# Retention attention and top-1 MoE on one core: score products on array quarters without the masked quarter, value halves swapped by ScalarE, head weights loaded two chunks later

## The chip, the cores and the metric

One Trainium2 chip, of which the kernel uses 1 core. The metric is device microseconds of one execution, as the median of the runs shown; a profile is one profiled execution with its own time. The engines are named as in the profile: PE is TensorE's matrix product and PEld its load of weights, ACT is ScalarE, DVE is VectorE, POOL is GpSimd, and SP (SyncE) issues most transfers. A line Lnnn is a line of the kernel.

## The reference

Four batches of eight heads, 768 positions, head size 64: a decaying linear attention with a causal recurrence. Its output, 3072 rows of 512, goes into a mixture of eight experts, of which each row uses the one with the largest logit.

```python
gamma = 1.0 - 2.0 ** (-5.0 - np.arange(H))            # one decay per head
for t in range(S):
    state = gamma[None, :, None, None] * state + np.einsum('bhd,bhe->bhde', k[:, :, t], v[:, :, t])
    y[:, :, t] = np.einsum('bhd,bhde->bhe', q[:, :, t], state) / np.sqrt(D)

x = y.transpose(0, 2, 1, 3).reshape(B * S, H * D)     # 3072 x 512
logits = x @ w_gate;  e_idx = argmax(logits)          # 8 experts
gate_w = softmax(logits)[e_idx];  eom = sigmoid(x @ w_output_gate)
out[row] = gate_w * eom[e_idx] * (relu(x @ w1[e_idx]) @ w2[e_idx])   # 512 -> 1024 -> 512
```

## The kernel before

The attention is done in chunks of 128 positions. There are 24 of them: chunk i is batch i // 6, position c = i % 6 in it. Queries are laid out for blocks of 256 positions, n = i // 2, so that an even chunk is the first and an odd one the second of its block. Within a chunk the recurrence is written as products: scores of each key with each query, a mask that keeps the keys which are not behind the query, scores times values, and, for c > 0, the query times the state that the chunk before left. The decay is put into the values and into a scale of the result (`gv`, `gq`).

`attend(i, between, before_state)` is one chunk. On TensorE it does, in this order:

- the scores `s` (L331): for each of four head pairs g and each half hh, keys (64 features by 128 keys) with 128 queries, in fp32, which takes two passes. Two such products stand beside each other in the array, each on a half of its rows (64*128 in the profile). VectorE multiplies the result with the mask into `am` (L335), 128x512 for each half hh;
- the carry-in (L348): the state `sd` with the queries, on array quarters (64*64), into `py`. It is left out where c = 0;
- what `between` holds: for even chunks the routing logits of the block before (`logits`, L379, whose result ScalarE copies as `lt`, L382), the transposes of the next chunk's keys (`kt_block`, L286, copied by ScalarE in L288) and of queries (`qt_block`, L304 and L305), then, for even chunks, transposes of the logits (L404) with the routing on VectorE (`route1`, L406 to L421) and an exponential on ScalarE (L425), for odd ones the counting products (L460, L461); and `tokens(i - 3)` (L453), the transposes `px` of finished rows;
- scores times values, onto `py` (L353), and the new state `st` (L361), both on column halves (128*64). The state isn't needed for c = 5.

Then `before_state` puts work of other blocks on the engines: gates of the block before (odd chunks), `build_row(i - 3)`, of which ScalarE writes the row (L506), and `qr_block(i + 3)`, by which ScalarE rearranges queries (L295). Behind it ScalarE copies the state as `sd` (L365) for the next chunk's carry-in, and VectorE multiplies `py` with `gq` into `yt` (L369). There is one buffer for `py`, so the next carry-in waits for `yt`. GpSimd makes the decayed values `vs` (`prep_v(i + 2)`, L281), parts of the rows, and scatters finished rows to memory, sorted by expert (L513).

From chunk 12 on, halves of the first expert's weights are loaded (`load_weights`, at the chunks in the table `w_at`) and, two and three chunks later, split into a high and a low part (`split_weights`: two casts on ScalarE, L176 and L177, two subtractions on GpSimd, L180 and L181). Behind the chunks the first 256 rows of the most frequent expert are computed on TensorE between the last pieces of routing (the head: `head_load`, L577, and `run_head`, L609 and L627), and then come the eight experts (L877, L895).

The order of instructions on PE, ACT, DVE and POOL is the order in which the code is written (`manual_schedule`). Each engine takes its own instructions strictly in that order; only the order of SP's transfers is set by a scheduler.

Of the kernel before, what the change touches and what calls it, by code (L numbers as in the profile page):

```python
# [32 lines left out]
def retention_moe_kernel(  # L33
# [40 lines left out]
    mask = cpool.tile([P, P], F32, name="mask")  # L74
    nc.gpsimd.memset(mask, 1.0)
    nc.gpsimd.affine_select(out=mask.rearrange("p (r m) -> p r m", r=2), in_=mask.rearrange("p (r m) -> p r m", r=2),
                            pattern=[[1, 2], [2, P // 2]], compare_op=ALU.is_ge,
                            fill=0.0, base=0, channel_multiplier=-1)
# [42 lines left out]
    wgs = cpool.tile([2 * NG, P * E], F32, name="wgs")  # L121
# [71 lines left out]
    with ExitStack() as actx:  # L193
# [88 lines left out]

        def kt_block(i):
# [30 lines left out]
        def attend(i, between, before_state):  # L314
# [10 lines left out]
            pss = []  # L325
            for hh in range(2):
                pss.append(ps_s.tile([P, NG, P], F32, name=f"s{hh}", tag="s"))
            for g in range(NG):
                for hh in range(2):
                    r = slice(hh * 64, hh * 64 + 64)  # L330
                    nc.tensor.matmul(rm(pss[hh][:, g]), kt[i][r, g], qc(r, g), start=True, stop=True)  # L331
            am = []
            for hh in range(2):
                a = ap.tile([P, NG, P], F32, name=f"am{hh}", tag=f"am{hh}", bufs=1)
                nc.vector.tensor_tensor(out=a, in0=pss[hh], in1=mask.unsqueeze(1).broadcast_to([P, NG, P]), op=ALU.mult)  # L335
                am.append(a)
# [14 lines left out]
            for g in range(NG):  # L351
                for hh in range(2):
                    nc.tensor.matmul(yo(g, hh), vs[i][:, 2 * g + hh], am[hh][:, g],  # L353
                                     start=(c == 0 and g % 2 == 0), stop=True, skip_group_check=True)
# [8 lines left out]
            before_state()  # L363
            if c < NC - 1:
                nc.scalar.copy(sd[(i + 1) % 2], st)  # L365
            kn.pop(i), vs.pop(i), kt.pop(i)
# [198 lines left out]
        w_at = {12: 0, 14: 2, 16: 4, 18: 6}  # L565
# [8 lines left out]
        def head_load():  # L574
            t = hpool.tile([P, HEAD // 32, SEG], F32, name="xl0")
# [78 lines left out]
        kt_block(0)  # L654
        qr_block(0)
# [10 lines left out]
        for i in range(NCH):  # L666
# [24 lines left out]
            def between():  # L691
# [35 lines left out]
            def before_state():  # L727
                if i == 0:
                    qr_block(2)
# [4 lines left out]
                if i >= 3:  # L734
                    build_row(i - 3)
                if i + 3 < NCH:
# [42 lines left out]
        flush(len(backlog))  # L779

# [326 lines left out]
```

## Time and profile before

| | |
|---|---|
| runs | 444.99, 446.6, 446.89 us |
| median | 446.6 us |
| the profiled execution: its time | 447.45 us |
| the profiled execution: its span | 445.7 us |
| chunks 0 to 2 | 0 to 31.4 us |
| chunks 3 to 23 | 31.4 to 138.0 us |
| the head | 138.0 to 168.6 us |
| the experts | 168.6 to 445.7 us |
| VectorE's mask product (L335) | 48 of 686 ns |
| the copy of the state (L365) | 20 of 375 ns |
| GpSimd's product `vs` (L281) | 24 of 1049 ns |
| casts of weights (L176, whole kernel) | 64 of 621 ns |

A row of the timeline gives the start of a group of like instructions, its busy time, engine, line, operation, output and inputs, the tile of the array (PE), the shapes, the number of instructions, and in brackets how long the engine stood idle before and what ended that. A group of several starts with its first and is busy until its last ends, so that the next may start before it is over: how far two starts lie apart says how long a group keeps its engine. A row of the waits gives the waiting engine and line, what it waited for, the total in us, the number of waits and the longest.

### The profile page before, as it was taken

To read this page: it belongs to the slowest core of one execution; us is meant where nothing else is said; L and a number is where in the kernel's file an instruction comes from. 1 tells how busy PE (TensorE), PEld (TensorE's weight loads), DVE (VectorE), ACT (ScalarE), POOL (GpSimd) and SP (SyncE) were. 2 spreads that over 40 slices of the span, in tenths; PEclk is the share of its full clock that TensorE was granted. 3 is DMA by queue.
4 is the path that set the end of the run, shared out by engine and by line. 5 is a ranking of instruction groups with operands and counts; after the bars stand their busy time and mean duration, and the time that the engine had idled before them with its cause. 6 is when DMAs were issued, how large, how long until landed. Compare 5 with 4: busy or idle time off the path is not lost.

```text
span 445.7 us, 9948 instructions
## 1 busy us (share of the span) xinstructions
PE 429.4 (96%) x3586; PEld 394.8 (89%) x3586; DVE 252.9 (57%) x675; ACT 191.3 (43%) x392; POOL 187.5 (42%) x242
## 2 busy tenths in 40 slices
PE   8999999999999998999999999999999999999993
PEld 4888778777877898999999999999999999999882
DVE  1357766766777538564745475476476476476111
ACT  3235555567764223543533453353343453454111
POOL 4433166458988305106005702711730740720722
PEclk9979999999999999899999999999999999999999
DMA  8949999999951277358444834943953863870102
GB/s 199 231 110 259 240 265 300 273 272 245 266 136 73 82 152 212 128 173 212 128 131 136 223 103 136 252 138 103 247 174 95 219 208 96 224 197 4 54 13 71
DMA packets 110068, 75.52 MB, mean 169 GB/s; under 512 B 55459, under 2 KB 97447, under 8 KB 110008
## 3 DMA queue, kind: packets, MB, share of 16 engines
q1 hardware_dynamic: 104720, 62.03, 54.6%
q0 software_dynamic: 5120, 12.69, 8.7%
q8 instruction: 30, 0.49, 0.5%
q14 instruction: 30, 0.25, 0.2%
q10 hardware_dynamic: 168, 0.06, 0.1%
HBM read 59.41 MB, written 15.83 MB: 169 GB/s over the span
## 4 chain that ended last, share of the span: by engine, by line
issue 44%; POOL 14%; PE 3%; DMA 2%; DVE 0%; POOLq 0%
POOL out_dram L185 14%; PE a L627 2%; PE h L609 1%; DMA out_dram<-ot,idi 1%; DMA out_dram<-ot,idx 1%; DVE ot L639 0%; POOLq L185 0%; DVE a L829 0%; DVE tj L802 0%; DVE no L803 0%; POOLq L979 0%
## 5 line engine op out<-in xcount | busy, mean ns | idle before, releaser
L185 POOL DMA_INDIRECT out_dram<-ot,idi x84 | 88.6, 1055 | 157.1 <-DVE ot L901 133.7
L877 PE MATMUL h<-xh,whi 128*128 128x224 f32 (+7 forms) x256 | 86.3, 337 | 0.0
L877 PE MATMUL h<-xw,whi 128*128 128x224 f32 (+7 forms) x256 | 86.2, 337 | 0.0
L877 PE MATMUL h<-xh,wlo 128*128 128x224 f32 (+7 forms) x256 | 86.2, 337 | 0.0
L895 PE MATMUL a<-hh,whi 128*128 128x224 f32 (+6 forms) x224 | 75.5, 337 | 1.1 <-ACT hh L881 1.1
L895 PE MATMUL a<-hl,whi 128*128 128x224 f32 (+6 forms) x224 | 75.7, 338 | 0.3 <-DVE hl L882 0.3
L895 PE MATMUL a<-hh,wlo 128*128 128x224 f32 (+6 forms) x224 | 75.5, 337 | 0.0
L180 DVE TENSOR_TENSOR wlo<-raw,whi 128x512 fp32r<-128x512 f32 x56 | 38.3, 684 | 58.8 <-ACT whi L176 55.8
L176 ACT CAST whi<-raw 128x512 fp32r<-128x512 f32 x64 | 39.8, 621 | 70.7 <-PE a L895 69.0
L882 DVE SCALAR_TENSOR_TENSOR hl<-h,hh 128x224 fp32r<-128x224 f32 (+7 forms) x64 | 34.9, 546 | 55.7 <-ACT hh L881 55.7
L881 ACT ACTIVATE hh<-h 128x224 fp32r<-128x224 f32 (+7 forms) x64 | 30.9, 485 | 79.2 <-PE h L877 79.1
L877 PEld LDWEIGHTS h<-xh,whi 128*128 128x128 f32 x256 | 48.6, 190 | 0.8
L877 PEld LDWEIGHTS h<-xw,whi 128*128 128x128 f32 x256 | 48.5, 190 | 0.7
L877 PEld LDWEIGHTS h<-xh,wlo 128*128 128x128 f32 x256 | 48.5, 189 | 0.5
L895 PEld LDWEIGHTS a<-hh,whi 128*128 128x128 f32 x224 | 42.6, 190 | 1.7 <-ACT hh L881 1.2
L895 PEld LDWEIGHTS a<-hl,whi 128*128 128x128 f32 x224 | 42.6, 190 | 1.0 <-DVE hl L882 0.5
L895 PEld LDWEIGHTS a<-hh,wlo 128*128 128x128 f32 x224 | 42.6, 190 | 0.4
L177 ACT CAST whi<-raw 128x512 fp32r<-128x512 f32 x64 | 39.5, 618 | 0.0
L513 POOL DMA_INDIRECT srt<-row,posi x24 | 24.5, 1019 | 33.4 <-ACT sd L365 11.1
L281 POOL TENSOR_TENSOR vs<-vn,gv 128x512 f32<-128x512 f32 x24 | 25.2, 1049 | 31.4 <-DMA vn<-in_v_dram 16.3
L181 DVE TENSOR_TENSOR wlo<-raw,whi 128x512 fp32r<-128x512 f32 x56 | 38.3, 684 | 0.0
L335 DVE TENSOR_TENSOR am<-s,mask 128x512 f32<-128x512 f32 x48 | 30.9, 686 | 9.8 <-PE s L331 9.8
(168 smaller groups left out, 667.4 us busy)
## 6 DMA issues: line engine op xcount, KB each, us to landing
raw<-in_moe_w_dram SPq DMA_DIRECT2D x32, 512.0 KB
raw<-in_moe_w_dram SPq DMA_DIRECT2D x32, 256.0 KB
raw<-in_moe_w_dram SPq DMA_DIRECT2D x64, 128.0 KB
kn<-in_k_dram SPq DMA_DIRECT2D x24, 256.0 KB
qn<-in_q_dram SPq DMA_DIRECT2D x12, 512.0 KB
vn<-in_v_dram SPq DMA_DIRECT2D x24, 256.0 KB
srt<-zrow SPq DMA_DIRECT2D x8, 325.0 KB
xl<-srt SPq DMA_DIRECT2D x12, 211.2 KB
```

What stands on the lines that cost most here:

```text
L176: nc.scalar.copy(cols(hi), r1)
L177: nc.scalar.copy(perm(hi), r2)
L180: eng.tensor_sub(cols(lo), r1, cols(hi).bitcast(F32))
L181: eng.tensor_sub(perm(lo), r2, perm(hi).bitcast(F32))
L185: st = nc.gpsimd.indirect_dma_start(out=dst, out_offset=bass.IndirectOffsetOnAxis(ap=idx, axis=0), in_=src, in_offset=None, bounds_check=n ...
L281: nc.gpsimd.tensor_mul(vs[i], vn.pop(i), gv[:, c, :].unsqueeze(2).broadcast_to([P, H, D]))
L335: nc.vector.tensor_tensor(out=a, in0=pss[hh], in1=mask.unsqueeze(1).broadcast_to([P, NG, P]), op=ALU.mult)
L513: st = nc.gpsimd.indirect_dma_start(out=srt, out_offset=bass.IndirectOffsetOnAxis(ap=posi, axis=0), in_=row, in_offset=None, bounds_check= ...
L877: nc.tensor.matmul(ps[:, 0:C], l[:, 0, w], r[:, dc, 0:C], start=(n == 0), stop=(n == 3 * NDC - 1))
L881: nc.scalar.activation(hh, ps[:, 0:C], AF.Relu)
L882: nc.vector.scalar_tensor_tensor(out=hl, in0=ps[:, 0:C], scalar=0.0, in1=hh.bitcast(F32), op0=ALU.max, op1=ALU.subtract)
L895: nc.tensor.matmul(accs[d][:, 0:C], l[:, 1, w], r, start=(f == 0 and n == 0), stop=(f == NF - 1 and n == 2))
```

## The change

**Scores.** The 128 keys and 128 queries of a chunk are cut into halves of 64. Early queries with late keys are masked altogether, and that quarter isn't computed any more. Early keys (z = 0) are multiplied with all 128 queries, late keys (z = 1) with the late 64 only, all on array quarters (64*64), 16 products in place of 8. For the head pairs 2 and 3 the two key halves land on swapped partitions (`half`). The result takes six blocks of 64 columns, the mask three, and VectorE's product is 128x384 in place of 128x512.

**Values.** The late queries take all 128 keys on column halves (64 columns each). The early queries take the early 64 keys only, on quarters, and come behind the state. Since half of the heads have their keys on swapped partitions, they need their values swapped in the same way: `swap_v` makes `vw`, two copies of 64x256 on ScalarE for each chunk. `before_state` moves behind the early queries' products (but for the last chunk, where it stays and a product of 8 columns, `pd`, is added).

**Order.** `swap_v(i + 1)` stands between `row` and `qr`, so ahead of `sd`, in ScalarE's order; that for chunk 0 stands ahead of the first `qr` and `qt` copies. Chunks 1 and 2 get a product of 8 columns each (`pd`). The table `w_at` moves by two chunks, and the last half's split goes behind the last scatters. The staging tile of the gate weights shares its buffer with the head's first tokens.

```diff
-    mask = cpool.tile([P, P], F32, name="mask")
+    mask = cpool.tile([P, 3, 64], F32, name="mask")
     nc.gpsimd.memset(mask, 1.0)
-    nc.gpsimd.affine_select(out=mask.rearrange("p (r m) -> p r m", r=2), ...
+    for half, x, n in ((0, 0, 1), (0, 2, 1), (1, 0, 2)):
+        m = mask[half * 64:half * 64 + 64, x:x + n].rearrange("p b (r m) -> p b r m", r=2)
+        nc.gpsimd.affine_select(out=m, in_=m, pattern=[[0, n], [1, 2], [2, 32]], compare_op=ALU.is_ge,
+                                fill=0.0, base=0, channel_multiplier=-1)
...
+        def swap_v(i):
+            vw[i] = ap.tile([P, H // 2, D], F32, name="vw", tag="vw", bufs=2)
+            for hf in range(2):
+                nc.scalar.copy(vw[i][64 * hf:64 * hf + 64], vs[i][64 - 64 * hf:P - 64 * hf, H // 2:])
+        def value(i, h):
+            return vs[i][:, h] if h < H // 2 else vw[i][:, h - H // 2]
...
-            for g in range(NG):
-                for hh in range(2):
-                    r = slice(hh * 64, hh * 64 + 64)
-                    nc.tensor.matmul(rm(pss[hh][:, g]), kt[i][r, g], qc(r, g), start=True, stop=True)
+            for g in range(2):
+                for z in range(2):
+                    for gg in (g, g + 2):
+                        for hh in range(2):
+                            r = slice(hh * 64, hh * 64 + 64)
+                            p = half(gg, z)
+                            if z == 0:
+                                out_ = pss[hh][p, g:gg + 3:gg + 2 - g].rearrange("p h (r m) -> p h r m", r=2)
+                                nc.tensor.matmul(out_, kt[i][r, gg, z * 64:z * 64 + 64], halves(qc(r, gg)), ...)
+                            else:
+                                nc.tensor.matmul(rm(pss[hh][p, gg + 2]), kt[i][r, gg, z * 64:z * 64 + 64], halves(qc(r, gg))[:, 1], ...)
...
             between()
-                    nc.tensor.matmul(yo(g, hh), vs[i][:, 2 * g + hh], am[hh][:, g],
-                                     start=(c == 0 and g % 2 == 0), stop=True, skip_group_check=True)
+                    nc.tensor.matmul(halves(rm(yo(g, hh)))[:, 1], value(i, 2 * g + hh), rm(am[hh][:, 2 + g]),
+                                     start=(c == 0 and g % 2 == 0), stop=False, skip_group_check=True)
...
-            before_state()
+            if i == NCH - 1:
+                before_state()
+                nc.tensor.matmul(ps_t.tile([P, NG, P], F32, name="pd", tag="t")[:, 0, 0:E], ident, ident[:, 0:E], start=True, stop=True)
+            for g in range(2):
+                for gg in (g, g + 2):
+                    for hh in range(2):
+                        p = half(gg, 0)
+                        nc.tensor.matmul(halves(rm(yo(gg, hh)))[:, 0], value(i, 2 * gg + hh)[p], rm(am[hh][p, g]),
+                                         start=False, stop=True, skip_group_check=True)
+            if i < NCH - 1:
+                before_state()
             if c < NC - 1:
                 nc.scalar.copy(sd[(i + 1) % 2], st)
...
-        w_at = {12: 0, 14: 2, 16: 4, 18: 6}
+        w_at = {14: 0, 16: 2, 18: 4, 20: 6}
...
         kt_block(0)
+        swap_v(0)
         qr_block(0)
...
+                if 0 < i < 3:
+                    pd = ps_t.tile([P, NG, P], F32, name="pd", tag="t")
+                    nc.tensor.matmul(pd[:, 0, 0:E], ident, ident[:, 0:E], start=True, stop=True)
...
             def before_state():
                 if i == 0:
+                    swap_v(1)
...
                 if i >= 3:
                     build_row(i - 3)
+                if 0 < i < NCH - 1:
+                    swap_v(i + 1)
                 if i + 3 < NCH:
                     qr_block(i + 3)
...
         flush(len(backlog))
+        split_weights(NF - 1)
```

The order of instructions, first on ScalarE from an even chunk's exponential (L425) to the first copy of the odd chunk behind it, before:

```order
L425 ACTIVATE misc<-misc 128x16
L506 ACTIVATE row<-px,gate 128x4x4x32
L295 COPY qr<-qn 128x512
L365 COPY sd_193<-st 128x256
L445 ACTIVATE ez<-z 128x2
L288 COPY kt<-pk 128x512
```

And the same place of the changed kernel, where the exponential is L468, the row L549, the queries' copy L310 and the state's L408:

```order
L468 ACTIVATE misc<-misc 128x16
L549 ACTIVATE row<-px,gate 128x4x4x32
L293 COPY vw<-vs 64x256 x2
L310 COPY qr<-qn 128x512
L408 COPY sd_195<-st 128x256
L488 ACTIVATE ez<-z 128x2
L303 COPY kt<-pk 128x512
```

The two swaps stand between the row and the queries' copy; nothing else changes its place there.

On TensorE, from the end of an even chunk's values (L353; the numbers behind `am` and `s` tell the two halves hh apart) over the state to the next scores, before:

```order
L353 MATMUL py<-am_959,vs 64x128
L353 MATMUL py<-am_961,vs 64x128
L361 MATMUL st<-vs,kn 64x64 x8
L331 MATMUL s_1057<-qt,kt 128x128
L331 MATMUL s_1058<-qt,kt 128x128
```

And in the changed kernel, from the last of the late queries' values (L385) over the state (L393) to the first four of the eight products of the early queries (L403), behind which the next scores (L358 and L361) follow:

```order
L385 MATMUL py<-am_895,vw 64x2x32
L385 MATMUL py<-am_897,vw 64x2x32
L393 MATMUL st<-vs,kn 64x64 x8
L403 MATMUL py<-am_895,vs 64x2x32
L403 MATMUL py<-am_897,vs 64x2x32
L403 MATMUL py<-am_895,vw 64x2x32
L403 MATMUL py<-am_897,vw 64x2x32
```

The early queries' products are now the last of a chunk that write `py`, behind the state, where before the state was last.

More of the change, by code (lines that the diff above doesn't have):

```diff
@@ L120, in retention_moe_kernel @@
     nc.scalar.dma_start(dcs, dec_c)
-    wgs = cpool.tile([2 * NG, P * E], F32, name="wgs")
+    wgs = hpool.tile([2 * NG, P * E], F32, name="wgs", tag="xl0")
     for j, w in enumerate((w_gate, w_ogate)):
@@ L281, in prep_v @@
             nc.gpsimd.tensor_mul(vs[i], vn.pop(i), gv[:, c, :].unsqueeze(2).broadcast_to([P, H, D]))
+        vw = {}
+        def swap_v(i):
[4 more added lines that the diff above has]
+            return vs[i][:, h] if h < H // 2 else vw[i][:, h - H // 2]
         def kt_block(i):
@@ L323, in qc, with half, halves @@
                 return qt[n][r, g, :, own]
-            pss = []
-            for hh in range(2):
-                pss.append(ps_s.tile([P, NG, P], F32, name=f"s{hh}", tag="s"))
-            for g in range(NG):
-                for hh in range(2):
-                    r = slice(hh * 64, hh * 64 + 64)
-                    nc.tensor.matmul(rm(pss[hh][:, g]), kt[i][r, g], qc(r, g), start=True, stop=True)
+            def half(g, h):
+                h = h if g < 2 else 1 - h
+                return slice(64 * h, 64 * h + 64)
+            def halves(t):
+                return t.rearrange("p r (h m) -> p h r m", h=2)
+            pss = [ps_s.tile([P, 6, 64], F32, name=f"s{hh}", tag="s") for hh in range(2)]
+            for g in range(2):
[6 more added lines that the diff above has]
+                                out_ = pss[hh][p, g:gg + 3:gg + 2 - g].rearrange("p h (r m) -> p h r m", r=2)
+                                nc.tensor.matmul(out_, kt[i][r, gg, z * 64:z * 64 + 64], halves(qc(r, gg)), start=True, stop=True,
+                                                 skip_group_check=True)
+                            else:
+                                nc.tensor.matmul(rm(pss[hh][p, gg + 2]), kt[i][r, gg, z * 64:z * 64 + 64], halves(qc(r, gg))[:, 1],
+                                                 start=True, stop=True, skip_group_check=True)
             am = []
             for hh in range(2):
-                a = ap.tile([P, NG, P], F32, name=f"am{hh}", tag=f"am{hh}", bufs=1)
-                nc.vector.tensor_tensor(out=a, in0=pss[hh], in1=mask.unsqueeze(1).broadcast_to([P, NG, P]), op=ALU.mult)
+                a = ap.tile([P, 6, 64], F32, name=f"am{hh}", tag=f"am{hh}", bufs=1)
+                nc.vector.tensor_tensor(out=a.rearrange("p (x b) m -> p x b m", b=2), in0=pss[hh].rearrange("p (x b) m -> p x b m", b=2),
+                                        in1=mask.unsqueeze(2).broadcast_to([P, 3, 2, 64]), op=ALU.mult)
                 am.append(a)
@@ L362, in attend @@
                                          start=(c == 0 and g == 0), stop=True, skip_group_check=True)
-            before_state()
+            if i == NCH - 1:
[9 more added lines that the diff above has]
+                before_state()
             if c < NC - 1:
                 nc.scalar.copy(sd[(i + 1) % 2], st)
-            kn.pop(i), vs.pop(i), kt.pop(i)
+            kn.pop(i), vs.pop(i), vw.pop(i), kt.pop(i)
             if h2 == 0:
@@ L574, in head_load @@
         def head_load():
-            t = hpool.tile([P, HEAD // 32, SEG], F32, name="xl0")
+            t = hpool.tile([P, HEAD // 32, SEG], F32, name="xl0", tag="xl0")
             for a in range(4):
```

3 lines of the change are left out of this document (removed).

## The prediction

> **What bounds the kernel now.** I read the busy line of the page first, then busy time by stretch, then the timeline of two chunks on TensorE, ScalarE and VectorE, and last the waits. The page makes TensorE look like the only limit:
>
> ```profile
> PE 429.4 (96%) x3586; PEld 394.8 (89%) x3586; DVE 252.9 (57%) x675; ACT 191.3 (43%) x392; POOL 187.5 (42%) x242
> ```
>
> By stretch (columns: length, then busy time of PE, PEld, DVE, ACT, POOL, then the granted clock, the DMA share and GB/s), chunks 3 to 23 and the experts behind them read alike. The change touches only the stretch up to 138 us; what follows is full of TensorE work and starts later or earlier as a whole.
>
> ```profile
> 0.00:31.40 31.40, 28.84 (x262) 21.89 (x262) 9.49 (x29) 9.56 (x20) 12.10 (x35) 0.89 0.88 187
> 31.40:138.00 106.60, 102.50 (x1546) 83.87 (x1544) 76.97 (x289) 63.76 (x143) 65.73 (x94) 1.00 0.93 242
> 168.60:445.70 277.10, 268.73 (x1514) 261.51 (x1512) 150.70 (x291) 108.98 (x207) 100.39 (x95) 0.99 0.52 146
> ```
>
> ScalarE has 40% idle time there, but the waits of that stretch (total, times, longest) show that TensorE's carry-in product waits for ScalarE's copy `sd` of the state about once in every second chunk:
>
> ```profile
> PEld py L348 <- ACT sd L365: 3.2, 11, 0.5
> ```
>
> The timeline shows where. TensorE in chunk 8 (even, scores at 57.37), then in chunk 9 (odd), up to chunk 10's carry-in:
>
> ```profile
> 57.37 1.16 PE L331 MATMUL s<-qt,kt 64*128 64x128 f32 x16
> 58.46 0.67 PE L348 MATMUL py<-qt,sd 64*64 64x128 f32 x16
> ...
> 60.56 0.38 PE L404 MATMUL misc<-ident,lt 128*128 128x128 f32 x2
> 61.02 0.66 PE L453 MATMUL px<-ident,yt 128*128 128x128 f32 x4
> 61.60 1.09 PE L353 MATMUL py<-am,vs 128*64 128x128 f32 x16
> 62.52 0.63 PE L361 MATMUL st<-vs,kn 128*64 128x64 f32 x16
> 63.09 1.16 PE L331 MATMUL s<-qt,kt 64*128 64x128 f32 x16
> 64.31 0.67 PE L348 MATMUL py<-qt,sd 64*64 64x128 f32 x16
> 64.90 0.66 PE L286 MATMUL pk<-ident,kn 128*128 128x128 f32 x4
> ...
> 66.23 0.66 PE L453 MATMUL px<-ident,yt 128*128 128x128 f32 x4 [0.20 <-ACT kt L288]
> 66.82 1.09 PE L353 MATMUL py<-am,vs 128*64 128x128 f32 x16
> 67.74 0.63 PE L361 MATMUL st<-vs,kn 128*64 128x64 f32 x16
> 68.31 1.16 PE L331 MATMUL s<-qt,kt 64*128 64x128 f32 x16
> 69.40 0.67 PE L348 MATMUL py<-qt,sd 64*64 64x128 f32 x16
> ```
>
> And ScalarE in the same time:
>
> ```profile
> 62.71 0.17 ACT L425 ACTIVATE misc<-misc 128x16 f32<-128x16 f32 x1 [1.26 <-PE py L353]
> 62.79 0.69 ACT L506 ACTIVATE row<-px,gate 128x512 f32<-128x512 f32 x1
> 63.36 0.62 ACT L295 COPY qr<-qn 128x512 f32<-128x512 f32 x1
> 63.87 0.39 ACT L365 COPY sd<-st 128x256 f32<-128x256 f32 x1
> 64.13 0.22 ACT L445 ACTIVATE ez<-z 128x2 f32<-128x2 f32 x1
> 65.60 0.59 ACT L288 COPY kt<-pk 128x512 f32<-128x512 f32 x1 [1.24 <-PE pk L286]
> 66.08 0.59 ACT L305 COPY qt<-pq 128x512 f32<-128x512 f32 x1
> 66.98 0.70 ACT L506 ACTIVATE row<-px,gate 128x512 f32<-128x512 f32 x1 [0.31 <-DVE misc L486]
> 67.56 0.61 ACT L295 COPY qr<-qn 128x512 f32<-128x512 f32 x1
> 68.42 0.37 ACT L365 COPY sd<-st 128x256 f32<-128x256 f32 x1 [0.25 <-PE st L361]
> ```
>
> In the even chunk ScalarE runs back to back from the exponential at 62.71 to the end of `sd` at 64.26, and the carry-in starts at 64.31. The exponential itself waits for VectorE's routing, whose last step is the `acc` row:
>
> ```profile
> 62.38 0.22 DVE L421 SCALAR_TENSOR_TENSOR acc<-misc,wm,acc 128x8 bf16<-128x8 f32 x1
> 62.75 0.69 DVE L369 TENSOR_TENSOR yt<-py,gq 128x512 f32<-128x512 f32 x1 [0.15 <-PE py L353]
> ...
> 67.97 0.69 DVE L369 TENSOR_TENSOR yt<-py,gq 128x512 f32<-128x512 f32 x1 [0.21 <-issue]
> ```
>
> 62.60 plus 0.11 is 62.71; the profile names `py`, which landed at the same time. So the even-to-odd passage, from transposes at 60.56 over VectorE and ScalarE to the carry-in, is a chain beside TensorE, and TensorE is 0.2 to 0.5 us ahead of it. In the odd chunk `sd` ends at 68.79 and TensorE arrives at 69.40: there TensorE sets the pace.
>
> **The change on TensorE.** Scores, values and state start at 63.09 (less 62.52), 62.52 (less 61.60) and 58.46 (less 57.37): values 0.92, state 0.57, scores 1.09, sum 2.58. The eight rounds of 128 columns of the values give about 0.11 each, the eight of 64 columns of the state about 0.06 each plus some 0.09 for the change of array form behind them; the carry-in rows are quarters already and give 0.11 for a round of four (0.44 of the 0.59 to 64.90). After: scores in four rounds of 128 and four of 64 columns, 0.68; late values in eight rounds of 64, 0.48; state 0.48; a change of form, 0.15 (63.09 less the last state record); early values in four rounds of 64, 0.24. Sum 2.03, so **0.55 us less TensorE time in a full chunk**. It is a gain only where TensorE is last.
>
> **The swaps on ScalarE** add two copies of 256 columns per chunk, between `row` and `qr`, ahead of `sd`. A 256-wide copy held the next one back 63.87 to 64.13 = 0.26; half of a 512-wide copy with an SBUF source, 63.36 to 63.87, is 0.255; half the partitions buys nothing on VectorE, and I assume the same here:
>
> ```profile
> L259 DVE COPY wg<-po 64x16 f32<-64x16 f32 x4 | 0.7, 183 | 0.1
> L257 DVE COPY wg<-po 128x16 f32<-128x16 f32 x2 | 0.4, 184 | 4.3 <-POOL gq L263 4.3
> ```
>
> The bounds of one swap are 0.13 (half as much, if partitions did count) and 0.51 (the full 512-wide step); I take 0.28, near the 256-wide row, with 0.02 for a source on other partitions. The Trainium skill, page "ScalarE: Activation LUTs", section "What ACT_TABLE_LOAD costs", prices an ACTIVATE with immediates at 186 ns plus 0.833 ns per column, with 93 ns of overlap back to back: an estimate from it is 0.31 per copy, and the first term below would be 6.1 in place of 5.6. The trace's 0.26 for the `sd` copy lies a little below that.
>
> *Even to odd.* From the px transposes to the next carry-in is 64.31 − 61.02 = 3.29 now, all of it beyond 62.71 on ScalarE. Nothing of the change makes the exponential earlier (its inputs come from `logits`, ahead of the values). So it becomes 3.29 + 2 × 0.28 = 3.85, while TensorE needs only 0.58 + 0.48 + 0.48 + 0.15 + 0.24 + 0.68 = 2.61: the 0.55 won there turns into waiting. For chunks 4, 6, … 22: 10 × 0.56 = **+5.6**. Chunk 2 has no row yet: **+0.2**.
>
> *Odd to even.* Now 69.40 − 66.23 = 3.17 by TensorE. After: the last early value lands at 0.59 + 0.48 + 0.48 + 0.15 + 0.24 + 0.17 = 2.11 past px; `yt` follows 0.06 later, takes 0.69 and frees the one `py` buffer, 0.06 on: 2.92. ScalarE: `row` at 0.75, 0.57 to the swaps, 0.56 for them, 0.51 for `qr`, 0.39 and 0.04 for `sd`: 2.82. So the gain is 0.25, not 0.55; seven such passages: **−1.75**. At the ends of sequences behind chunks 5 and 17, where no `sd` follows, about 0.18 each, **−0.4**; behind 11 VectorE's choice of the expert is last, 0.
>
> **The start.** `swap_v(0)` stands ahead of the first qt copies on ScalarE and waits for GpSimd's first `vs`:
>
> ```profile
> 8.31 1.04 POOL L281 TENSOR_TENSOR vs<-vn,gv 128x512 f32<-128x512 f32 x1 [3.50 <-DMA vn<-in_v_dram]
> 8.75 1.07 ACT L305 COPY qt<-pq 128x512 f32<-128x512 f32 x2 [0.49 <-PE pq L304]
> ```
>
> `vs` ends at 9.35, so the copies go from 8.75 to about 9.9; some of that was spare: +0.6 at most. Chunks 0 to 2 are TensorE-bound at a clock of 0.89 on average, partly half speed, and save two to three times 0.4 to 0.6 there: I take **−0.3** (between −0.9 and +0.6).
>
> **The end of the stage.** Chunk 23 gets a dummy product and two more changes of form and splits the values with little to win: **+0.35** (0 to 0.5). The other edits cost nothing: the mask is made by GpSimd in the 3.50 us wait of the row above; VectorE's mask product is 384 instead of 512 wide, 0.55 against 0.69 by width, and wasn't last; the dummy products of chunks 1 and 2 are 8 columns wide. Weight loads two chunks later move casts too, about 1.03 us of ScalarE per chunk. They stand behind `ez` or, in odd chunks, behind `sd`, as these of an even chunk do now, and end 0.2 us ahead of the next `kt`, which moves back with them:
>
> ```profile
> 128.80 0.61 ACT L176 CAST whi<-raw 128x512 fp32r<-128x512 f32 x1
> 130.15 0.59 ACT L288 COPY kt<-pk 128x512 f32<-128x512 f32 x1 [0.21 <-PE pk L286]
> ```
>
> The last raw load (1 MB) is now queued on SP behind the head's token loads
>
> ```profile
> 128.25 1.95 SPq L577 DMA_DIRECT2D xl<-srt  x4
> ```
>
> and at the 242 GB/s of that stretch would take 4.3 us: I put its landing near 136 and its first cast at about 139.5. If that cover of 3 us goes, each us late is a us late at the head.
>
> **Sum.** 5.6 + 0.2 − 1.75 − 0.4 − 0.3 + 0.35 = +3.7. The profiled execution took 447.45 (span 445.7 and 1.75 around it), 0.85 above the median 446.6. Scaled to the median: **450.3 us**, slower.
>
> **Rivals.**
>
> *TensorE is the bound after all* (faster). The place is the even-to-odd passage: if the swaps and about 0.7 us more leave the chain exponential–`row`–`qr`–`sd` (`row` starting ahead of the exponential's wait, say), 0.55 × 21 = 11.5 comes off: 435. It decides as soon as that chain is under the 2.61 of TensorE. For it speaks the 96% of the busy line; against it the order of ScalarE's queue and the 11 waits on `sd`. Even at swaps for nothing 450.3 − 5.8 = 444.5 is left, inside no change. The Trainium skill, page "TensorEngine Tiling (Array Packing)", section "Theoretical Speedup", has up to 2x for a dimension of 64 or less, which points this way; its section "PSUM Bottleneck" says that other engines' copies may become the limit once tiling has sped TensorE up, which the waits on `sd` here bear out. Chance 0.10.
>
> *The terms cancel* (no change). A swap at 0.13 makes the first term 2.6; with the start at −0.9 the sum is 0.1, so 446 to 448.8. Chance 0.18.
>
> *GpSimd is late with `vs`.* The swap for chunk i+1 waits on ScalarE for the product that GpSimd makes for it:
>
> ```profile
> 60.85 1.07 POOL L281 TENSOR_TENSOR vs<-vn,gv 128x512 f32<-128x512 f32 x1
> ```
>
> Its end, 61.92, lies 1.4 us ahead of the swap at 63.36. If GpSimd's rows, scatters and casts' remainders push it past that in five chunks by 0.5 to 1 us, the sum grows by 2.5 to 5: 453 to 455.5. Against it: that is the closest of the steady chunks. Chance 0.12.
>
> **How the numbers follow.** The forecast has 0.60. With it I count rounds of 64 columns that turn out as long as those of 128: then the odd gain is lost and the time is 452.4. Swaps at 0.51 would give 450.3 + 10 × 0.46 = 454.9; swaps at 0.255 with the start at −0.9 give 449.2. The range takes in these and most of the two neighbours: 446.0 to 455.5. A measurement of this kernel can tell about 0.5% (2.2 us) from no change: faster is below 444.4, slower above 448.8. Faster 0.10 (the first rival), same 0.20 (the second and the low edge of the forecast), slower 0.70.
>
> **What would show it.** The carry-in of odd chunks waits on `sd` some 0.7 to 1.2 us (0.2 to 0.5 now) in ten chunks; even-to-odd passages are 3.85, odd-to-even 2.9 with a wait on `yt`; TensorE's busy time between 31 and 138 falls by about 10 us while the stretch grows; two `vw` copies spaced 0.28 stand ahead of each `qr`. It is wrong if the copies are spaced under 0.15, if the wait on `sd` doesn't grow, if the exponential starts earlier after px than 1.69 us, or if the granted clock in the stretch, 1.00 now, falls because TensorE idles more.

## The result, and the profile after

The changed kernel takes 462.0 us (median; 460.5 to 462.4) against 445.8 for the kernel before on the same chip: a ratio of 1.036, 95% interval 1.032 to 1.040. Slower was right; 450.3 with a range up to 455.5 was too low. The profiled execution took 460.5 us with a span of 458.7, so it is 13.1 us over that of before. The medians lie 16.2 us apart, because that execution of before was 1.65 us above its median and this one 1.5 below; what follows divides the 13. A ratio leaves out executions that took over 1.5% longer than the fastest of their kernel, and a median counts all.

TensorE is busy 7.9 us less than before, and ScalarE 20.7 us more:

```profile
PE 421.5 (92%) x4360; PEld 386.6 (84%) x4360; DVE 245.2 (53%) x675; ACT 212.0 (46%) x440; POOL 187.3 (41%) x244
```

The starts of the first score product of a chunk and of the last product of the head divide the 13 us:

| | before | after | difference |
|---|---|---|---|
| chunk 0 | 10.49 | 12.12 | +1.6 |
| chunk 3 | 31.37 | 34.01 | +2.6 |
| chunk 23 | 137.98 | 150.07 | +12.1 |
| last product of the head | 168.47 | 182.68 | +14.2 |
| end | 445.7 | 458.7 | +13.0 |

So 9.5 us are lost in chunks 3 to 22, 2.6 ahead of them and 2.1 behind; 1.2 come back in the experts, where the profile of before has 3.4 us at half clock (from 177.5) that this one hasn't. By stretch (same columns as before), TensorE now has 19% idle time in the chunks, where it had 4%:

```profile
0.00:34.00 34.00, 29.75 (x360) 22.39 (x364) 8.52 (x28) 12.18 (x26) 12.68 (x37) 0.85 0.82 172
34.00:150.00 116.00, 94.49 (x2192) 76.45 (x2186) 70.50 (x288) 79.00 (x177) 60.53 (x90) 1.00 0.84 223
```

The waits of that stretch name what it waits for. The same wait had a total of 3.2 us before:

```profile
PEld py L380 <- ACT sd L408: 19.0, 16, 1.7
DVE yt L412 <- PE py L403: 11.2, 18, 0.8
```

The timeline of chunk 8 (odd-to-even passage into it, 60.85 to 64.05) and chunk 9 (even-to-odd, 66.60 to 70.85) shows both kinds of passage on TensorE, from the transposes px (now L496) to the next carry-in (now L380):

```profile
60.85 0.66 PE L496 MATMUL px<-ident,yt 128*128 128x128 f32 x4 [0.21 <-ACT kt L303]
61.43 0.45 PE L385 MATMUL py<-am,vs 128*64 128x64 f32 x8
61.95 0.64 PE L393 MATMUL st<-vs,kn 128*64 128x64 f32 x16
62.80 0.40 PE L358 MATMUL s<-qt,kt 64*64 64x128 f32 x8
63.35 0.29 PE L361 MATMUL s<-qt,kt 64*64 64x64 f32 x8
64.05 0.67 PE L380 MATMUL py<-qt,sd 64*64 64x128 f32 x16 [0.40 <-ACT sd L408]
66.60 0.65 PE L496 MATMUL px<-ident,yt 128*128 128x128 f32 x4
70.85 0.67 PE L380 MATMUL py<-qt,sd 64*64 64x128 f32 x16 [1.46 <-DVE am L366]
```

And ScalarE in the same two passages:

```profile
61.54 0.69 ACT L549 ACTIVATE row<-px,gate 128x512 f32<-128x512 f32 x1 [0.26 <-PE px L496]
62.26 0.82 ACT L293 COPY vw<-vs 64x256 f32<-64x256 f32 x2
63.10 0.62 ACT L310 COPY qr<-qn 128x512 f32<-128x512 f32 x1
63.63 0.37 ACT L408 COPY sd<-st 128x256 f32<-128x256 f32 x1
...
68.29 0.17 ACT L468 ACTIVATE misc<-misc 128x16 f32<-128x16 f32 x1 [1.26 <-DVE acc L464]
68.37 0.69 ACT L549 ACTIVATE row<-px,gate 128x512 f32<-128x512 f32 x1
69.08 0.82 ACT L293 COPY vw<-vs 64x256 f32<-64x256 f32 x2
69.91 0.62 ACT L310 COPY qr<-qn 128x512 f32<-128x512 f32 x1
70.44 0.37 ACT L408 COPY sd<-st 128x256 f32<-128x256 f32 x1
```

In both, ScalarE goes back to back from `row` to `sd`, and the carry-in starts when `sd` ends (64.00, 70.81). At 70.85 the profile names VectorE's `am`, which runs until 71.28 and can't have been it; the weight load of the same product names `sd`:

```profile
70.85 0.43 PEld L380 LDWEIGHTS py<-qt,sd 64*64 64x64 f32 x16 [1.59 <-ACT sd L408]
```

The even-to-odd passage went from 3.29 to 4.25 us (+0.96), the odd-to-even one from 3.17 to 3.20. From `row` to `qr` is 1.54 us, where it was 0.57: **the two copies cost 0.97 us**, not 0.56.

### The profile page after: what moved, and what is told of

Read it like the earlier page. It is cut to its first block, busy times and chain, and to the rows that moved or that the text cites. A ratio compares the mean times of both kernels' runs of the same rounds, so it can differ in the third digit from the quotient of the medians.

```text
span 458.7 us, 11543 instructions
## 1 busy us (share of the span) xinstructions
PE 421.5 (92%) x4360; PEld 386.6 (84%) x4360; DVE 245.2 (53%) x675; ACT 212.0 (46%) x440; POOL 187.3 (41%) x244
## 4 chain that ended last, share of the span: by engine, by line
issue 43%; PE 15%; POOL 12%; DMA 12%; ACT 9%; DVE 7%; SPq 1%; POOLq 0%; ACTq 0%; DVEq 0%
POOL out_dram L189 12%; DMA out_dram<-ot,idi 5%; DMA srt<-row,posi 4%; PE py L380 3%; PE pk L301 3%; ACT kt L303 2%; PE px L496 2%; ACT vw L293 2%; ACT row L549 2%; PE py L385 2%; ACT qr L310 1%; DMA vn<-in_v_dram 1%; DVE yt L412 1%; PE misc L422 1%; PE st L393 1%
## 5 line engine op out<-in xcount | busy, mean ns | idle before, releaser
L285 POOL TENSOR_TENSOR vs<-vn,gv 128x512 f32<-128x512 f32 x24 | 25.1, 1046 | 35.5 <-PE py L403 13.4
L380 PE MATMUL py<-qt,sd 64*64 64x128 f32 x320 | 13.7, 288 | 19.3 <-ACT sd L408 10.2
```

Source lines behind the costliest of these rows:

```text
L285: nc.gpsimd.tensor_mul(vs[i], vn.pop(i), gv[:, c, :].unsqueeze(2).broadcast_to([P, H, D]))
L380: nc.tensor.matmul(rm(yo(gg, hh)), sd[i % 2][r, gg], qc(r, gg), start=(g == 0), stop=False, skip_group_check=True)
```

## The experiments

Each is compared with the kernel before on its own chip. Those chips differ: the kernel before took 445 us on two of them and 472 to 480 on the others, where waits for memory come in, above all between chunks 7 and 10 and in the experts. Passages are therefore read in chunks without such waits. The first theory (S): ScalarE's copies lie on the chain to `sd`, and that chain sets the time. The rival (T): quarters and changes of form cost TensorE more than was counted.

**No copies**

```diff
-        swap_v(0)
...
-                    swap_v(1)
...
-                if 0 < i < NCH - 1:
-                    swap_v(i + 1)
...
-            return vs[i][:, h] if h < H // 2 else vw[i][:, h - H // 2]
+            return vs[i][:, h]
```

> The changed kernel without the two copies per chunk on ScalarE; heads 4 to 7 read their values with the halves in the old order, so that this part of the result is another one. Theory S (the copies sit on ScalarE's chain from the routing exponential to the copy of the state, and that chain sets the time): even-to-odd passages from px to the next carry-in go from 4.25 back to 3.29 us (ten of them, -9.6), odd-to-even ones from 3.20 to about 2.9 (-1.8 to -2), the start loses 1.6 to 2.3 and the last chunk 0.8: 462 becomes about 447 to 448, the value of before plus the rest. Theory T (array quarters and changes of form on TensorE cost more than counted, the copies little): no lower than 456.

Routing changes with the values, so that the total (524 us) can't be compared. The passages can; TensorE in chunks 12 and 13, up to the carry-in of chunk 14:

```profile
84.10 0.66 PE L496 MATMUL px<-ident,yt 128*128 128x128 f32 x4
87.42 0.67 PE L380 MATMUL py<-qt,sd 64*64 64x128 f32 x16 [0.53 <-DVE acc L482]
89.39 0.66 PE L496 MATMUL px<-ident,yt 128*128 128x128 f32 x4 [0.24 <-ACT kt L303]
92.43 0.62 PE L380 MATMUL py<-qt,sd 64*64 64x128 f32 x11 [0.23 <-DVE yt L412]
```

Even-to-odd is 3.32, as before the change (3.29), and odd-to-even 3.04, 0.13 less than before, with the wait on `yt` that the prediction had put there. S holds for the chunks: without the copies nothing is lost in a passage, and little is won.

**Copies without a shift, and one copy**

```diff
-                nc.scalar.copy(vw[i][64 * hf:64 * hf + 64], vs[i][64 - 64 * hf:P - 64 * hf, H // 2:])
+                nc.scalar.copy(vw[i][64 * hf:64 * hf + 64], vs[i][64 * hf:64 * hf + 64, H // 2:])
```

> Both copies of 64x256 per chunk stay, but each reads the partitions that it writes (no shift; heads 4 to 7 get their values unswapped). If a copy takes 0.41 us with no overlap because its input lies on other partitions, the copies are now spaced about 0.26 to 0.28 and the time falls by some 10 x 0.3 + 7 x 0.25 = 4 to 5 us, to about 457. If it is because they use 64 partitions, or because two such follow each other, nothing changes: 462 with spacings of 0.41.

```diff
-            for hf in range(2):
-                nc.scalar.copy(vw[i][64 * hf:64 * hf + 64], vs[i][64 - 64 * hf:P - 64 * hf, H // 2:])
+            nc.scalar.copy(vw[i], vs[i][:, H // 2:])
```

> One straight copy of 128x256 per chunk on ScalarE in the place of the two of 64x256; heads 4 to 7 get their values unswapped, and with them the routing and so the experts' part is another one, so that only the attention stage is compared. If the two copies cost 0.97 us per chunk because ScalarE doesn't overlap neighbours whose first partition differs (0, 64, 0), one copy from partition 0 overlaps on both sides: 0.26 between the starts of the copy and of the next one, and the even-to-odd passage is 3.29 + 0.26 = 3.55. If the price lies in the elements copied or in the wait on GpSimd, it is about half of 0.97 or the whole: 3.8 to 4.25.

ScalarE with two straight copies, from `row` to `qr`:

```profile
103.64 0.69 ACT L549 ACTIVATE row<-px,gate 128x512 f32<-128x512 f32 x1
104.22 0.80 ACT L293 COPY vw<-vs 64x256 f32<-64x256 f32 x2
105.04 0.62 ACT L310 COPY qr<-qn 128x512 f32<-128x512 f32 x1
```

And with one copy of 128 partitions:

```profile
89.05 0.69 ACT L548 ACTIVATE row<-px,gate 128x512 f32<-128x512 f32 x1
89.64 0.39 ACT L292 COPY vw<-vs 128x256 f32<-128x256 f32 x1
89.93 0.62 ACT L309 COPY qr<-qn 128x512 f32<-128x512 f32 x1
```

These two kernels compute other values and so another routing (totals 535.3 and 542.2 us), and again only the passages can be compared. Here is the one behind chunk 12, with the time from the start of `row` to that of `qr` on ScalarE:

| | `row` to `qr` | passage |
|---|---|---|
| before | 0.59 | 3.32 |
| no copies | 0.59 | 3.32 |
| one copy of 128x256 | 0.88 | 3.61 |
| two straight copies of 64x256 | 1.41 | 4.13 |
| two swapped copies (the change) | 1.54 | 4.27 |

The passage grows by what stands between `row` and `qr`, to 0.01 us. So the shift alone, the first cause that was offered, is worth 0.13; the rest is in the halves. One copy of 128x256 holds `qr` back by 0.29 us, though it is 0.39 long, because it overlaps with its neighbours. The measured starts fit one reading: **a copy whose first partition is another one than its neighbour's starts only when that one has ended**. In the change (input from 64, then from 0, then `qr` from 0 but written from 0 behind a copy written to 64) all three joints lose their overlap; straight copies lose two (`vw` starts 0.58 behind `row`, which is 0.69 long); one copy loses none. That is three of three cases, and not a rule tried further. Another fits them as well: nothing overlaps with a half copy ahead of it, and a copy to other partitions doesn't overlap with what is ahead of it. The Trainium skill, page "Advanced Engine Details and Errata", section "The Read-Write Bubble", says that ScalarE's accesses aren't pipelined between instructions; the trace bears this out for the halves (0.41 apart) and not for whole copies (0.29 apart at a length of 0.39).

**Copies behind the state's**

```diff
                 if i >= 3:
                     build_row(i - 3)
-                if 0 < i < NCH - 1:
-                    swap_v(i + 1)
...
                 out_gate(n1)
                 gates(n1)
+            if 0 < i < NCH - 1:
+                swap_v(i + 1)
```

> The changed kernel with the copies for chunk i+1 moved in ScalarE's order from ahead of the queries' copy to behind the copy of the state (and behind ez), for all chunks from the second on. Theory S: the even-to-odd passage goes back to 3.3 us and odd-to-even to 2.9, about -11 to -12 together with the last chunk's 0.8: about 450. In chunks with weight casts, ScalarE then has 0.83 + 1.03 us of work ahead of the next keys' copy, where before 0.2 us were free: up to 0.6 us for each of some four even chunks, so up to 452. Theory T: no change, 460 to 462.

Ratio 1.030 (1.023 to 1.037) on a chip where the kernel before took 471.7. Even-to-odd passages are back at 3.22 to 3.33 in most chunks, but the total isn't (450 us was expected, a ratio of 1.01): in chunks with weight casts ScalarE now has copies and casts ahead of the next `kt`, and px waits for it. The last row is px of the odd chunk 17:

```profile
111.36 0.82 ACT L293 COPY vw<-vs 64x256 f32<-64x256 f32 x2
112.20 0.62 ACT L180 CAST whi<-raw 128x512 fp32r<-128x512 f32 x1
112.73 0.61 ACT L181 CAST whi<-raw 128x512 fp32r<-128x512 f32 x1
113.25 0.58 ACT L303 COPY kt<-pk 128x512 f32<-128x512 f32 x1
```

```profile
113.88 0.66 PE L496 MATMUL px<-ident,yt 128*128 128x128 f32 x4 [0.97 <-ACT kt L303]
```

Chunk 23 starts at 145.25, and at 151.21 in the next run, which is on the same chip and has the change's order from chunk 2 on. What more of the 3% lies behind the chunks isn't known: there is no profile of the kernel before on that chip.

**The start**

```diff
         kt_block(0)
-        swap_v(0)
...
         qt_block(1)
+        swap_v(0)
...
-                    swap_v(1)
                     qr_block(2)
                     qt_block(2)
+                    swap_v(1)
```

> The changed kernel with the swaps of chunks 0 and 1 behind the first query copies on ScalarE in place of ahead of them. Theory S: the first scores, 1.63 us later than before the change, come back by 1.5 to 1.7 and those of chunk 2 by a further 0.5: 459.7 to 460.4. Rival: TensorE's stretch at half clock or the products of chunk 1 take the time back, no change within 0.3 us.

Ratio 1.036 (1.030 to 1.041), as for the change itself. The first scores do start 1.07 us earlier than those of the run before it on that chip (10.47 against 11.54), but chunk 3 starts at 31.76 against 31.91: the rival holds. What takes it back is the carry-in of chunk 1, which waits for `sd`, since the swaps for chunk 1 still stand ahead of that on ScalarE. The run before, then this one:

```profile
17.29 0.67 PE L380 MATMUL py<-qt,sd 64*64 64x128 f32 x16 [0.64 <-ACT sd L408]
```

```profile
17.12 0.67 PE L380 MATMUL py<-qt,sd 64*64 64x128 f32 x16 [1.59 <-ACT sd L408]
```

It isn't the clock: both have one stretch of 6.8 us at half clock there, from 20.9 and 20.8. In the changed kernel's own profile the clock does come in. ScalarE's first copies there, and TensorE's wait for them:

```profile
9.66 0.82 ACT L293 COPY vw<-vs 64x256 f32<-64x256 f32 x2 [1.52 <-POOL vs L285]
10.50 1.07 ACT L320 COPY qt<-pq 128x512 f32<-128x512 f32 x2
```

```profile
11.14 0.40 PE L246 MATMUL pm<-dcs,sel 2*128 2x24 f32 x2 [1.17 <-ACT qt L320]
```

and the granted clock (third from the end of a row) in the stretches that follow, after:

```profile
9.00:13.40 4.40, 3.23 (x48) 2.47 (x45) 1.09 (x4) 1.88 (x4) 1.46 (x2) 1.00 1.26 260
13.40:16.80 3.40, 3.24 (x51) 2.62 (x49) 0.78 (x2) 2.01 (x4) 2.07 (x3) 0.50 1.29 260
```

and before:

```profile
9.00:13.40 4.40, 3.94 (x38) 3.13 (x37) 2.13 (x5) 1.93 (x4) 1.40 (x2) 1.00 1.26 252
13.40:16.80 3.40, 3.02 (x54) 2.60 (x54) 1.13 (x2) 1.38 (x3) 2.04 (x2) 1.00 1.27 260
```

TensorE gets 3.4 us at half clock from 13.4 on, which before it didn't. From the first scores to those of chunk 1 it takes 5.24 us; with the copies behind the state's, where the order is the same up to there and the clock stays full, it takes 4.22. So the start lost twice: 1.6 us by the copies, and about 1.0 by the clock. The Trainium skill, page "TensorE: Matmul & The Clock Gate", section "What's actually happening", has such a window of 3413 ns that falls to half rate behind an idle one; 3.40 is the length here, but TensorE was busy for 3.23 of the 4.40 us ahead of it, far from idle. What makes the clock fall stays open, and it isn't the busy share that the profile shows: in the run with the later swaps TensorE was busy for less of such a stretch, 1.81 of 3.40 us, and the clock stayed full behind it.

```profile
13.80:17.20 3.40, 1.81 (x56) 1.43 (x57) 1.72 (x3) 2.28 (x5) 2.04 (x2) 1.00 1.22 256
17.20:20.60 3.40, 3.40 (x30) 3.06 (x30) 0.00 (x0) 0.59 (x1) 1.64 (x2) 1.00 1.00 238
```

**Copies on VectorE**

```diff
-                nc.scalar.copy(vw[i][64 * hf:64 * hf + 64], vs[i][64 - 64 * hf:P - 64 * hf, H // 2:])
+                nc.vector.tensor_copy(vw[i][64 * hf:64 * hf + 64], vs[i][64 - 64 * hf:P - 64 * hf, H // 2:])
...
                 am.append(a)
+            if i < NCH - 1:
+                swap_v(i + 1)
```

> The changed kernel with the swaps on VectorE, those for chunk i+1 behind the mask products of chunk i (1.4 to 1.8 us idle there), that of chunk 0 behind the first two query copies; nothing is left out. If ScalarE's copies were the whole loss, ScalarE's chain is that of before: even-to-odd passage 3.3, odd-to-even about 3.0 (bound by yt), the start as before; with 0.3 us for the last chunk's extra products and up to 0.7 at the head the ratio to before is 0.996 to 1.002. If the quarters on TensorE cost something as well, it stays over 1.01.

Ratio 1.042 (1.031 to 1.053), no better than on ScalarE. Two such copies on VectorE, first in chunk 5, then in chunk 18:

```profile
43.38 0.59 DVE L293 COPY vw<-vs 64x256 f32<-64x256 f32 x2
...
118.20 4.28 DVE L293 COPY vw<-vs 64x256 f32<-64x256 f32 x2
```

and GpSimd's work at the second place:

```profile
118.51 1.27 POOL L184 TENSOR_TENSOR wlo<-raw,whi 128x512 fp32r<-128x512 f32 x1
119.73 1.27 POOL L185 TENSOR_TENSOR wlo<-raw,whi 128x512 fp32r<-128x512 f32 x1
120.97 1.03 POOL L285 TENSOR_TENSOR vs<-vn,gv 128x512 f32<-128x512 f32 x1
```

With GpSimd idle a pair takes 0.59 us; while it works through three products without a pause, the pair ends 0.5 us behind the last of them, and the routing behind it on VectorE is late by 3.7 us. This test of S is therefore spoilt by a collision that it brought along itself. The next one has the same copies:

```diff
-            if i < NCH - 1:
-                before_state()
             if c < NC - 1:
                 nc.scalar.copy(sd[(i + 1) % 2], st)
+            if i < NCH - 1:
+                before_state()
```

> As e7_dve, and ScalarE copies the state ahead of the row and the queries, right behind the exponential. Then ScalarE's chain ends about 1.1 us earlier and the passage is bound by yt, 2.11 + 0.06 + 0.69 + 0.06 = 2.9 to 3.05 in both kinds of chunk: ten times -0.3 in the even ones on top of e7_dve, ratio to before 0.988 to 0.995. Rival: the row and the queries, now later on ScalarE, hold back the next transposes, and the ratio is that of e7_dve or above.

Ratio 1.034 (1.026 to 1.043): the collision (chunks 18 and 19 take 8.89 and 9.74 us) hides what it was made for. Its control, the kernel before with the same move:

> The kernel before with that one reordering (state copied ahead of row and queries), without any of the change. TensorE is last there, 0.1 to 0.3 us behind ScalarE's old end: -1 to -2 us, ratio 0.995 to 0.998. If it equals e8_dve_sd, the array quarters are worth nothing even when nothing hides them; if e8_dve_sd is lower by 1 to 3 us, that is their worth here, less than the 11.5 that TensorE's own time would give.

Ratio 1.0017 (0.9984 to 1.0050): no gain that the total shows, though the copy of the state ends 0.6 us ahead of the carry-in now and not 0.05. The even-to-odd passages are 3.17 in most chunks, as odd-to-even ones, where they were 3.23 to 3.33. So in the kernel before ScalarE was last behind even chunks by about 0.1 us, with TensorE close behind it.

**The change again, and the weight loads**

> The changed kernel once more, as the reference on the chip of this series. Ratio to before 1.03 to 1.04 as in the first comparison.

Ratio 1.038 (1.033 to 1.042), 462.5 us, with 444.8 for the kernel before.

```diff
-        w_at = {14: 0, 16: 2, 18: 4, 20: 6}
+        w_at = {12: 0, 14: 2, 16: 4, 18: 6}
...
         flush(len(backlog))
-        split_weights(NF - 1)
```

> The changed kernel with the weight loads back at chunks 12, 14, 16 and 18 (and no split behind the last scatters). If the later loads cost something (a passage at chunk 19 to 20 that is 0.5 us longer than its like, and 0.7 us more in the head, where two casts stand ahead of the expert's activations), this is 1 to 2 us under a0_after; on a chip whose memory is slower, more. If they were hidden as forecast: within 0.5 us of a0_after.

459.6 us, ratio 1.032 (1.027 to 1.037): the medians lie 2.9 us apart, and the two intervals overlap. In the profiles chunk 23 starts at 149.19 and 149.09, so nothing of it lies in the chunks, and a longer chunk 19 (6.86 and 6.85 us, where its like take 6.2) is in both. Their difference is behind, where the profile of the change has two stretches at half clock and that of this kernel one. Whether the loads or the clock make it stays open.

**Copies where ScalarE is idle**

```diff
+                if i > 0 and i % 2 == 0:
+                    swap_v(i + 1)
                 if n1 >= 0:
                     route1(n1)
...
-                if 0 < i < NCH - 1:
-                    swap_v(i + 1)
...
                 gates(n1)
+            if i % 2 == 1 and i < NCH - 1:
+                swap_v(i + 1)
```

Together with the start and the weight loads of the two kernels above:

> The changed kernel with ScalarE's swaps where ScalarE is idle: in even chunks ahead of the exponential, in odd ones behind the copy of the state; those of chunks 0 and 1 behind the first query copies; weight loads back at chunk 12. If the copies' place on ScalarE and these two are the whole loss, the even-to-odd passage is 3.3 us and the ratio to before 1.000 to 1.006 (the last chunk's products and the early part remain). If the array quarters cost something themselves, over 1.01.

447.9 us, ratio 1.0063 (1.0031 to 1.0094): 14.6 of the 17.7 us are back on the chip of the two runs above, so T falls, since every product on TensorE is that of the change. By the profiles the place of the copies does most of it: chunks 3 to 22 take 107.1 us, where the change takes 116.1 in both of its profiles and the kernel before 106.6. The earlier start gives nothing (chunk 3 starts at 33.42, in the change's profile of that chip at 33.11). Behind the start of chunk 23 it is 306.7 against 312.2 us, where the change has two stretches of 3.4 us at half clock, from 152.1 and 193.1, that this run hasn't. And with the copies' move alone:

> The changed kernel with nothing but ScalarE's swaps for chunks 2 to 23 moved to where ScalarE is idle (even chunks: ahead of the exponential; odd: behind the copy of the state); early part and weight loads as in the change. If the copies' place is the loss in the chunks and the start and the late weight loads are only small parts: 450 to 452 against 445 before and 462 as changed (about 10 to 11 of the 17 us). If the start or the loads were the larger part: over 455.

Ratio 1.018 (1.010 to 1.026) on a chip where the kernel before took 471.9. In the chunks up to 7, ahead of memory waits, its chunks are those of v1 (5.42, 5.69 and 4.81 from 3 to 6). By the ratio about half of the 3.7% comes back by the place of the copies alone; the medians, 477.7 and 471.9, lie 1.2% apart, and on that chip the runs of the kernel before spread by more than 2%, so that this share is uncertain. How much of the rest is the weight loads' and how much the clock's stays open.

**The state first, and casts out of the way**

> As v1_spread, with the state copied ahead of the row and the queries. Passages bound by yt, 2.9 to 3.05 us in both kinds of chunk: 2 to 4 us under v1_spread, ratio to before 0.990 to 0.999. Rival: row and queries, later on ScalarE, push the casts into the next chunk's key copies, and nothing is won over v1_spread.

445.5 us, ratio 1.0026 (0.9992 to 1.0059). The pair of chunks 7 and 8, without casts, takes 4.99 + 5.61 = 10.60, before 5.15 + 5.72 = 10.87; those with casts take up to 6.07 each. Chunks 3 to 22 are 107.1 us in all, as without the move: what chunks without casts win, those with casts lose. The profile is 3.4 us shorter, and that lies ahead of chunk 3 (it starts at 29.98 against 33.42), where the other had 3.4 us more at half clock. So the odd chunks' casts are moved ahead of the state's copy, where ScalarE has 1.35 us idle:

```diff
                     qt_block(i + 2)
+                if i - 3 in w_at:
+                    split_weights(w_at[i - 3] + 1)
...
-            for z in range(2):
-                if i - 2 - z in w_at:
-                    split_weights(w_at[i - 2 - z] + z)
+            if i - 2 in w_at:
+                split_weights(w_at[i - 2])
```

> As v2_spread_sd (ratio 1.003), and the odd chunks' weight casts moved into the 1.3 us that ScalarE waits for the state there. In v2_spread_sd the chunks with casts took 5.6 to 6.1 us where those without took 5.0 and 5.6, about 3 us in all. If the casts on ScalarE are the cause, those chunks come back to 5.0 and 5.6 and the ratio to before is 0.993 to 0.998. If it is something else (gaps inside TensorE's groups, GpSimd), it stays at 1.000 to 1.004.

and the control, the kernel before with the last two moves:

> The kernel before with the same two moves (state copied first, odd casts ahead of it) and none of the change: control for v3_casts. TensorE is last there: ratio 0.995 to 1.000. If v3_casts is under it by 0.3% or more, the array quarters have a worth of their own once the swaps are off the chain; if not, none that can be measured.

0.9939 (0.9888 to 0.9989) and 1.0002 (0.9939 to 1.0064); again, on another chip:

> v3_casts once more, since the chip of the last series spread by 2% and the intervals of v3_casts and its control overlap. Quarters with a worth of their own: ratio 0.992 to 0.997, and chunks without casts at 5.0 (odd) and 5.6 us (even), with casts the same. None: 0.998 to 1.003.

> b3_before_casts once more, the control: 0.996 to 1.001, at least 0.3% over v3_again if the quarters have a worth, equal to it if not.

0.9878 (0.9819 to 0.9936) and 0.9996 (0.9965 to 1.0026). The intervals of this version lie under 1 in both series, and those of its control don't. Set against the control itself, the first series doesn't tell the two apart (the intervals overlap, the medians are 467.7 and 468.6), and the second does (476.3 and 480.7). Its passages in chunks 3 and 4 (odd-to-even, then even-to-odd):

```profile
33.67 0.66 PE L496 MATMUL px<-ident,yt 128*128 128x128 f32 x4 [0.20 <-ACT kt L303]
36.80 0.67 PE L380 MATMUL py<-qt,sd 64*64 64x128 f32 x16 [0.33 <-DVE yt L412]
...
39.36 0.66 PE L496 MATMUL px<-ident,yt 128*128 128x128 f32 x4
42.49 0.67 PE L380 MATMUL py<-qt,sd 64*64 64x128 f32 x16 [0.33 <-DVE misc L476]
```

Both are 3.13 and follow `yt`, which VectorE ends at 36.65 and 42.34:

```profile
35.96 0.69 DVE L412 TENSOR_TENSOR yt<-py,gq 128x512 f32<-128x512 f32 x1 [0.76 <-PE py L403]
41.65 0.69 DVE L412 TENSOR_TENSOR yt<-py,gq 128x512 f32<-128x512 f32 x1 [0.78 <-PE py L403]
```

From chunk 6 on most of them, of both kinds, are 3.06, where the control's are 3.17, TensorE's own pace: 0.11 us won a passage. The odd chunks with casts aren't back at the 5.0 us that were expected (chunk 15 takes 5.65). By the starts of chunks 4 to 7, 5.69, 4.59 and 5.00 stand against 5.72, 4.64 and 5.12 in the control. In the last series chunk 23 starts at 139.91 and 140.22, and the head ends at 171.0 and 171.1 in both: up to there the two are level. The experts, which the change doesn't touch, take 301.5 and 308.7, of which up to 3.4 are the clock's, since the control has two more stretches of 3.4 us at half clock there; in the series before, the experts were the other way about. So the 1.2% of that series isn't shown to be the quarters', and where it comes from isn't settled.

## Why the prediction was right or wrong

The spans put the forecast's terms beside what was measured (starts of chunks; for chunk 22 the carry-in behind it, for chunk 23 and the head what is left of the +14.2):

| | forecast | measured |
|---|---|---|
| even to odd, behind chunks 4, 6, … 22 | +5.6 | +10.2 |
| behind chunk 2 | +0.2 | +0.95 |
| odd to even and ends of sequences | −2.15 | −0.6 |
| the start | −0.3 | +2.6 |
| chunk 23 and the head | +0.35 | +1.0 |
| the experts | 0 | −1.2 |
| sum | +3.7 | +13.0 |

- **What bounds: right.** The carry-in behind even chunks follows `sd`, and `sd` follows ScalarE's row of instructions from the exponential. The exponential starts 1.69 us after px, as predicted. TensorE was less far ahead of it than the 0.2 to 0.5 us that were read, about 0.1 by the run that moves the state alone. That it came out slower is no luck: the wait for `sd` grew where it was said to grow, from 3.2 to 19.0 us, and without the copies the passage was back.
- **TensorE's saving: right.** Late values 0.52 (0.48 forecast), state with the change of form 0.57 (0.63), early values 0.28 (0.24), scores to the start of their last group 0.55. It bought no time because TensorE isn't last.
- **The price of a swap: this is the term that failed.** "half the partitions buys nothing on VectorE, and I assume the same here" took a half copy for a whole one. A whole one is spaced 0.29, very near the 0.28 taken, but two halves with another first partition overlap neither with each other nor with their neighbours: 0.97 a pair. The bounds, 0.13 to 0.51 each, did hold it (0.485); the value was chosen from the nearest row of another form. With it +5.6 became +10.2, and behind chunk 2, where 0.2 was taken, it came through whole. Even the upper bound, though, gave 454.9: the range failed by the next terms too. (0.5 us of the first line lie in chunk 19, with early and late loads alike, and come back in chunk 20, so in the third line.)
- **Odd to even: wrong as a consequence.** −0.25 each was forecast, bound by `yt`, with ScalarE 0.10 us behind that as the next limit. With 0.97 in the place of 0.56 ScalarE took over: +0.03 each in most of the seven passages, so that none of the 1.75 us came. With the copies away it was −0.13 and not −0.25, since `yt` starts 2.20 us behind px and not 2.17, and the carry-in follows 0.15 behind its end and not 0.06.
- **The start: wrong.** −0.3 was forecast and +2.6 measured. "some of that was spare" was not so: TensorE stood idle 1.17 us for the copies of qt, all of the 1.6 us came through, and a stretch at half clock, which no term had, came on top with about 1.0. With the copies later they stood ahead of chunk 1's `sd` and cost the same.
- **The last chunk and the head: too small.** The extra products and changes of form cost the 0.3 that was forecast (1.33 us against 1.03 for chunk 23's values). The remaining 0.7 of the head were not taken apart. The carry-in of chunk 23 comes 1.1 us later behind its scores (2.62 against 1.51); that is the swap ahead of `sd` again, and counted in the first line.
- **The weight loads: open.** They were costed at nothing; the chunks bear that out, the medians speak for up to 2.9 us.
- **The rivals.** TensorE as the bound was not it, nor the cancelled terms. ScalarE waited for GpSimd's `vs` once, 1.5 us at the start, and not in chunks 3 to 23.

## What to carry to other kernels

An engine with 57% idle time can hold the only chain that matters: before work is put on it, look for the stretch in which it runs back to back into something that the bounding engine waits for, and put the work into its gaps instead. Take an operation's price from a row with its own shape and partitions, neighbours included, since what a copy costs in a full queue is its spacing and not its length. And once TensorE is sped up, the next limits (here `sd`, then `yt`) decide what is left of it: 0.55 us saved in a chunk became 0.11 in the best version here.

## What the hardware showed unexpectedly

ScalarE spaces copies of 128x256 by 0.29 us, and copies of 64x256 on changing halves by 0.41 with the overlap at both ends gone, although each moves half as much (48 copies of 0.40 to 0.41 us in the changed kernel). VectorE's copy of two such halves took 0.59 us alone and up to 4.3 us beside a busy GpSimd; its mask product, 1.01 for two, is not held up in the same chunks. And TensorE's clock fell to half for 3.4 us behind a stretch in which it was busy 73% of the time (3.23 of 4.40 us), while in another run it stayed full behind one with 53% (1.81 of 3.40).
